# Attention and MoE on one core: other PSUM banks for the score blocks, transposes and value products, and weight passes at other places

## Chip, cores and metric

The kernel runs on one core of one Trainium2 chip. The metric is the device time of one execution in microseconds (us). The time before is the median of three runs.

## What is computed

Attention over 4 batches, 8 heads, 576 positions and head size 64, with a bias that a small network makes from relative positions, and behind it a two-layer MLP with a rational activation. Cut to what matters:

```python
scores = scale * q @ k.transpose(0, 1, 3, 2)
x = (psi_rel / psi_i)[..., None]
bias = maximum(x @ w1 + b1, 0) @ w2
scores = scores + bias.transpose(2, 0, 1)[None]
attn = exp(scores - max(scores)); attn = attn / (sum(attn) + 1e-9)
x = (attn @ v) as [2304, 512]
h = x @ w_in                                 # 512 -> 2048
g = (a0 + a1*h + a2*h^2 + a3*h^3) / (1 + |b0|*|h| + |b1|*h^2 + 1e-6)
out = g @ w_out                              # 2048 -> 512
```

## The kernel before

**Stages.** First the bias tables are made (to about 49 us), 36 groups `n` of 16 rows: rectified rows on VectorE and ScalarE, products with w2 on TensorE (L769), a read-out by ScalarE (L775), and a DMA to DRAM, from which bias tiles are read back. Then attention (to about 275 us), then the MLP. All of PSUM is one tile `W` of 8 banks with 512 columns of fp32; a helper `on` (L99) tells the dependency tracker which banks an instruction touches, so that waits between engines go by bank. Every engine works in the order in which the program is written; nothing reorders it.

**Attention.** A pair of heads of one batch is a unit (16 of them), and 128 query rows of it are a step; the last 64 rows of two units make one step together, so that there are 72 steps. A step `i` has two score blocks, `j` = 0 and 1, one per head, of 128 rows and 576 columns. `rnd(r)` (L599) writes one round: the scores of steps `i` = 2r and `i+1`, and what follows for the steps `i-1`, `i-2` and `i-3`:

- `e_qk` (L335): score products q·k (L346), two per block. The heads lie on different halves of the rows of the array and are woven together. A block is 576 wide and a bank 512, so before the change a block lay in a strip across two banks (`strip`, L332), cut into 448 and 128 columns; the four strips of a round shared banks 4 and 1.
- `e_ttr` (L359): the reduction. VectorE adds the bias to the score block and takes the row extreme in one custom instruction (L365), followed by a read of its accumulator. It writes `s2` and `m`.
- `e_exp` (L373): exponentials on ScalarE (L380), from `s2` to `prob`.
- `e_tp` (L426): transposes of `prob` on TensorE (L432), 16 `main` ones and 2 `ends` (the last 64 columns) per step, and, for units that end, `adds` (their row sums). `copy` (L446) brings the main ones from PSUM to `pt` by ScalarE (L447); `put_tails` (L454) brings ends and sums to `tl` and `rt` by VectorE.
- `e_pv` (L480): value products (L491), 20 per step, and `put` (L498), by which VectorE copies the output from PSUM to `xs` (L500).

A round's order on TensorE is: scores, transposes of step i-2, transposes of i-1, value products of i-3, value products of i-2.

**Weight passes.** Rounds 4 to 33 also split the MLP's weights into a high and a low part, two jobs `a` and `b` in every three rounds (`job_plan`, L567; phase `ph`): the mask pass `mag` (L156, VectorE), `rebias` (L165, ScalarE), `sign` (L168, VectorE), `mid` (L177, GpSimd), `join` (L181, VectorE), `low` (L188, GpSimd), and stores of the high part (`hi`) and the low one (`out`). `plan` says at which place of the round each is written:

```python
if ph == 0:
    plan.update(first=a[1], act=a[2], pool2=[a[4]], third=[a[3][0], hi(a)])
elif ph == 1:
    plan.update(first=b[1], act=b[2], second=[a[3][1]], pool2=[a[3][2]], outs=[out(c)])
else:
    plan.update(
        first=[b[3][0]], pool=[b[4]], second=[b[3][1]], pool2=[b[3][2]],
        outs=[hi(b), out(c + 1)],
    )
```

Here `a[1]` is mag, `a[2]` rebias, `a[3]` = sign, join, low, store, and `a[4]` mid. `first` stands ahead of the reductions of step i, behind the last put; `second` between the reductions of i and those of i+1; `third` and `outs` at the round's end.

**Start and end.** `start(0)` and `start(1)` (L662) write scores, reductions and exponentials of steps 0 and 1 behind the table groups y = 33 and y = 35. `finish` (L670) writes the last transposes and products and the first product of the MLP.

Of the kernel before, what the change touches and what calls it, by code (L numbers as in the profile page):

```python
# [37 lines left out]
def tile_attn_moe(  # L38
# [194 lines left out]
    with tc.manual_schedule():  # L233
# [3 lines left out]
        with ExitStack() as actx:  # L237
# [89 lines left out]
            MAIN_A, MAIN_B = 128, S - 128  # L327

            def low_first(i, j):
                return (i + j) % 2 == 0  # L330

            def strip(i, j):  # L332
                return 3 * 512 * (1 - j) + (512 - MAIN_B if low_first(i, j) else 1024 - MAIN_A)

            def e_qk(i):  # L335
# [6 lines left out]
                def product(j, a, z):  # L342
                    r, o0 = slice(64 * j, 64 * j + 64), strip(i, j)
# [6 lines left out]
                cuts = [(MAIN_A, S), (0, MAIN_A)], [(0, MAIN_B), (MAIN_B, S)]  # L350
                return [
                    [
                        (5 * (z - a) // 3, lambda j=j, a=a, z=z: product(j, a, z))
                        for a, z in cuts[low_first(i, j)]
                    ]
                    for j in range(2)
                ]

            def e_ttr(i, j):  # L359
                u, c = steps[i]  # L360
                p, b = units[u]
                t = epool.tile([P, S], F32, tag="s2", name=f"s2_{i}_{j}", bufs=4)
                m = epool.tile([P, 1], F32, tag="m", name=f"m{i}_{j}", bufs=8)
                o0 = strip(i, j)
                op = on(V.tensor_tensor_reduce(  # L365
                    out=t, in0=WF[:, o0:o0 + S], in1=bias[p][:, 5 * j + c, :],
                    scale=-0.125, scalar=3.0e38,
                    op0=ALU.add, op1=ALU.min, accum_out=m,
                ), o0 // 512, o0 // 512 + 1)
# [56 lines left out]
            def e_tp(i, to, tails, us=()):  # L426
# [11 lines left out]
                for r in range(2):  # L438
# [4 lines left out]
                    ends.append([op(r, tails[r], 128 + 64 * (i % 2), pb[:, 512:512 + P])])  # L443
                    adds.append([op(r, tails[r], 256, sums[u % 4]) for u in us])
# [9 lines left out]
            def put_tails(i, n, tails, us):  # L454
# [3 lines left out]
                for r, b in enumerate(tails):  # L458
                    on(V.tensor_copy(  # L459
                        out=t[:, k:k + n, 64 * r:64 * r + 64],  # L460
                        in_=W[:, b, 128 + 64 * k:128 + 64 * (k + n)].rearrange("p (k s) -> p k s", s=64),
                    ), b, mem=(f"tl{i // 2 % 2}",))
                for u in us:
# [3 lines left out]
                    for r, b in enumerate(tails):  # L467
                        on(V.tensor_copy(out=rt[0:n, 64 * r:64 * r + 64], in_=W[0:n, b, 256:320]), b)
# [98 lines left out]
            def job_plan(r):  # L567
                q, ph = divmod(r - 4, 3)
                c = 2 * q
                plan = {k: [] for k in ("first", "act", "pool", "second", "pool2", "third", "outs")}  # L570
# [26 lines left out]
            ZZ = (4, 1)  # L597

            def rnd(r):  # L599
# [21 lines left out]
                for j in range(2):  # L621
                    op = e_ttr(i, j)
                for x in plan["second"]:
                    op = x()
                for x in plan["pool2"]:
                    behind(x(), op)
# [25 lines left out]
                for x in plan["third"] + list(hi[1:]) + plan["outs"]:  # L652
                    x()
# [16 lines left out]
            def finish():  # L670
                run(puts)
                main, ends, _, copy = e_tp(NS - 2, (6, 7), ZZ)
# [8 lines left out]
                main, ends, adds, copy = e_tp(NS - 1, (5, 0), ZZ, us)  # L681
# [8 lines left out]
                put = e_pv(NS - 1, 5)  # L690
# [6 lines left out]
            with ExitStack() as bctx:  # L697
# [56 lines left out]
                for y, n in enumerate(order):  # L754
# [6 lines left out]
                    pa = (6, 7) if y == NG - 2 else (2 * ((y + 2) % 4), 2 * ((y + 2) % 4) + 1)  # L761
# [50 lines left out]
        with ExitStack() as mctx:  # L812
# [14 lines left out]
            def hb(s):  # L827
                return 2 - 2 * (s % 2), 3 - 2 * (s % 2)

            OB = (4, 5, 6, 7)  # L830
# [254 lines left out]
```

## Time and profile before

| | |
|---|---|
| median of three runs | 676.18 us (672.44 to 678.76) |
| the profiled execution | 674.15 us, span 672.4 us |
| TensorE busy (matmul) | 657.0 us, 98% of the span |
| VectorE busy | 554.0 us, 82% |
| ScalarE busy | 474.8 us, 71% |
| GpSimd busy | 153.2 us, 23% |
| granted TensorE clock | full speed in the whole span |

The profiled execution is 1.8 us longer than its span, which runs from the first to the last instruction. Matmuls are pipelined and overlap in the records, so a stop of TensorE appears as idle only in the part that is longer than the end of the matmul before it. Busy shares are means over the three stages; a round of attention has to be read by itself.

### The profile page before, as it was taken

Reading aid. Unit: us, or ns where it says so; the run is one execution under the profiler, and the core shown is the slowest. Engines: PE = TensorE matmul, PEld = TensorE weight load, DVE = VectorE, ACT = ScalarE, POOL = GpSimd, SP = SyncE. Lnnn points to the kernel's source line nnn. Section 1 sums busy time; section 2 is a strip of 40 time slices with the busy share of each in tenths; the row PEclk is TensorE's granted clock in tenths of the full one; section 3 lists DMA queues with packets and bytes.
Section 4 is the critical chain, followed back from the end, with each engine's and each line's share of the span. In section 5 each row is a group of like instructions: output and inputs, shape, how many; then the busy total and the mean of one; then the engine's idle time right before and its main releaser. Section 6 shows DMA issues by size and latency. Waiting matters only on the chain.

```text
span 672.4 us, 16098 instructions
## 1 busy us (share of the span) xinstructions
PE 657.0 (98%) x6274; PEld 537.2 (80%) x6274; DVE 554.0 (82%) x1030; ACT 474.8 (71%) x758; POOL 153.2 (23%) x108
## 2 busy tenths in 40 slices
PE   9999999999999899999999999999999999999997
PEld 6657777777777677988888888899988888888996
DVE  7986878788778787599998989979769878687776
ACT  7988898889889798566766657666655656455451
POOL 0000134333342321032221221221221212212211
PEclk9999999999999999999999999999999999999999
DMA  6887788677977974442662625768531301303031
GB/s 241 287 310 224 273 253 272 214 253 233 312 246 234 310 235 140 149 143 95 182 210 77 229 86 178 220 234 288 189 128 48 126 0 63 109 13 114 0 110 47
DMA packets 74844, 118.97 MB, mean 177 GB/s; under 512 B 11904, under 2 KB 33808, under 8 KB 74768
## 3 DMA queue, kind: packets, MB, share of 16 engines
q1 hardware_dynamic: 74624, 117.79, 53.0%
q8 instruction: 49, 0.80, 0.5%
q14 instruction: 27, 0.22, 0.1%
q10 hardware_dynamic: 144, 0.16, 0.1%
HBM read 79.17 MB, written 35.61 MB: 171 GB/s over the span
## 4 chain that ended last, share of the span: by engine, by line
PE 66%; DVE 4%; DMA 3%; issue 1%; ACT 1%; SPq 0%; DVEq 0%
PE ps L316 29%; PE ps L914 29%; PE ps L491 3%; DVE s L365 3%; PE ps L346 2%; PE ps L432 2%; DMA ws<-wh 2%; DMA wx<-in_w_out_dram 1%; DVE xs L500 0%; ACT p L380 0%; DVE tl L459 0%; ACT pt L447 0%; DVE sum L390 0%; DVE m L365 0%; DVE wk L156 0%
## 5 line engine op out<-in xcount | busy, mean ns | idle before, releaser
L884 POOL TENSOR_TENSOR gl<-m,r 128x1024 fp32r<-128x1024 f32 (+1 forms) x39 | 85.6, 2194 | 299.9 <-DVE m L877 243.9
L365 DVE CUSTOM_DVE_ANT_0 s<-ps,bias 128x576 f32<-128x576 f32 x144 | 105.6, 753 | 42.6 <-PE ps L346 33.2
L835 ACT ACTIVATE w<-ps,babs 128x1024 f32<-128x1024 f32 (+1 forms) x40 | 41.3, 1032 | 106.0 <-PE ps L316 102.3
L380 ACT ACTIVATE p<-s,m 128x576 f32<-128x576 f32 x144 | 110.1, 773 | 2.6 <-DVE m L365 2.6
L447 ACT COPY pt<-ps 128x512 f32<-128x512 f32 (+1 forms) x109 | 74.4, 727 | 22.7 <-PE ps L432 22.2
L346 PE MATMUL ps<-k,q 64*128 64x448 f32 (+3 forms) x640 | 89.8, 425 | 0.2 <-DVE m L365 0.2
L914 PE MATMUL ps<-wol,gh 128*128 128x512 f32 x216 | 84.2, 390 | 0.0
L914 PE MATMUL ps<-woh,gh 128*128 128x512 f32 x216 | 84.2, 390 | 0.0
L491 PE MATMUL ps<-pt,v 128*64 128x128 f32 (+1 forms) x1280 | 78.2, 265 | 1.8 <-ACT pt L447 1.8
L847 DVE SCALAR_TENSOR_TENSOR u<-w,babs,ps 128x1024 f32<-128x1024 f32 (+1 forms) x40 | 46.9, 1172 | 37.0 <-ACT t L836 36.8
L432 PEld LDWEIGHTS ps<-ident,p 64*128 64x128 f32 x1296 | 49.8, 138 | 28.0 <-DVE m L365 10.6
L491 PEld LDWEIGHTS ps<-pt,v 128*64 128x64 f32 x1280 | 65.1, 137 | 6.7 <-ACT pt L447 2.2
L316 PE MATMUL ps<-xb,wih 128*128 128x512 f32 (+1 forms) x240 | 68.7, 367 | 0.0
L842 ACT ACTIVATE u<-u 128x1024 f32<-128x1024 f32 (+1 forms) x40 | 39.1, 978 | 41.7 <-DVE u L847 41.5
L432 PE MATMUL ps<-ident,p 64*128 64x64 f32 x1296 | 55.0, 225 | 7.4 <-DVE m L365 6.4
L346 PEld LDWEIGHTS ps<-k,q 64*128 64x128 f32 (+1 forms) x640 | 43.5, 176 | 21.7 <-issue 16.6
L863 DVE SCALAR_TENSOR_TENSOR gh<-t,cst,r 128x1024 fp32r<-128x1024 f32 (+1 forms) x40 | 47.0, 1175 | 9.4 <-ACT r L844 7.0
L914 PE MATMUL ps<-woh,gl 128*128 128x512 f32 x216 | 53.8, 389 | 0.0
L870 DVE SCALAR_TENSOR_TENSOR m<-u,qc,gh 128x1024 f32<-128x1024 f32 (+1 forms) x40 | 47.1, 1178 | 5.1 <-DVE gh L863 1.4
L316 PEld LDWEIGHTS ps<-xb,wih 128*128 128x128 f32 x240 | 44.5, 188 | 6.0
L877 DVE SCALAR_TENSOR_TENSOR m<-t,cst,m 128x1024 f32<-128x1024 f32 (+1 forms) x40 | 47.1, 1178 | 1.4
L856 DVE SCALAR_TENSOR_TENSOR t<-t,cst,ps 128x1024 f32<-128x1024 f32 (+1 forms) x40 | 47.0, 1175 | 1.4
(81 smaller groups left out, 1319.8 us busy)
## 6 DMA issues: line engine op xcount, KB each, us to landing
tab<-e SPq DMA_DIRECT2D x36, 295.5 KB, 3.3
wx<-in_w_in_dram SPq DMA_DIRECT2D x16, 512.0 KB, 5.1
wx<-in_w_out_dram SPq DMA_DIRECT2D x16, 512.0 KB, 4.9
v<-in_vp_dram SPq DMA_DIRECT2D x16, 320.0 KB, 5.4
ws<-wh SPq DMA_DIRECT2D x20, 256.0 KB, 2.0
ws<-wl SPq DMA_DIRECT2D x20, 256.0 KB, 3.4
q<-in_qt_dram SPq DMA_DIRECT2D x16, 288.0 KB, 4.4
k<-in_kt_dram SPq DMA_DIRECT2D x16, 288.0 KB, 4.4
```

Source lines behind the costliest of these rows:

```text
L316: on(T.matmul(hps[s][:, j, :w_], w[:, k, sl], x[:, k, :w_], start=(k == 0 and z == 0), stop=(k == KD - 1 and z == 2),), b + j)
L346: on(T.matmul(WF[o, o0 + a:o0 + z], q[r, x], k[r, a:z], start=True, stop=True), (o0 + a) // 512)
L365: op = on(V.tensor_tensor_reduce(out=t, in0=WF[:, o0:o0 + S], in1=bias[p][:, 5 * j + c, :], scale=-0.125, scalar=3.0e38, op0=ALU.add, op1= ...
L380: A.activation(out=prob[i][:, z * S:z * S + S], in_=t, func=AF.Exp, bias=m, scale=-1.0, accum_out=sums[u % 4][:, k:k + 1],)
L432: on(T.transpose(W[:, b, o:o + 64], src[x, :], ident[x, x]), b)
L447: on(A.copy(out=t.rearrange("p x (r s) -> p r x s", r=2)[:, a:z], in_=W[:, to[a]:to[a] + z - a].rearrange("p r (x s) -> p r x s", s=64),), ...
L491: on(T.matmul(ps[y, o], vt[n][:, kc, y], w_, start=(kc == 0), stop=(kc == 4)), b, mem=(f"pt{i % 3}", f"tl{i // 2 % 2}"))
L856: on(V.scalar_tensor_tensor(out=rt[s, "t"], in0=rt[s, "t"], scalar=abs_[:, 1:2], in1=hp(s), op0=ALU.add, op1=ALU.mult,), *hb(s), mem="t")
L870: V.scalar_tensor_tensor(out=m, in0=rt[s, "u"], scalar=qc, in1=rt[s, "gh"].bitcast(F32), op0=ALU.add, op1=ALU.mult,)
L877: V.scalar_tensor_tensor(out=m, in0=rt[s, "t"], scalar=abs_[:, 0:1], in1=m, op0=ALU.add, op1=ALU.subtract)
L884: eng.tensor_tensor(out=lo, in0=rt[s, "m"], in1=rt[s, "r0"], op=ALU.mult)
L914: on(T.matmul(po[n, c], l[:, j, c * P:(c + 1) * P], r[fp][:, j, :], start=(first and x is a), stop=(last and x is z),), OB[c])
```

## The change

Each score block gets a pair of banks of its own, half of its columns (288) in each bank. `side(i)` gives the four banks of a step: one step of a round lies in banks 0 to 3, the other in 4 to 7, and the sides are swapped every round. With `b` the side of step i and `o` that of step i+1, the transposes of step i-2 go into (b, b+1) and those of i-1 into (b+2, b+3), which step i's reductions have read; tails and sums go behind the score columns of (o+1, o+3); the value products of i-3 and i-2 go into b+1 and b. All four score blocks stand at the round's start, both reductions of step i+1 stand ahead of the tail copies, and the places of the weight passes are four instead of seven. In the last two table groups, in `finish` and in the MLP only bank numbers change (MLP: first products in banks 0, 1 and 4, 5 instead of 0 to 3, second ones in 2, 3, 6, 7 instead of 4 to 7).

```diff
-                b = 2 - 2 * (s % 2)
+                b = 4 - 4 * (s % 2)
...
-            def strip(i, j):
-                return 3 * 512 * (1 - j) + (512 - MAIN_B if low_first(i, j) else 1024 - MAIN_A)
+            def side(i):
+                return 4 * ((i // 2 + i) % 2)
...
+                def product(j, a):
+                    r, b = slice(64 * j, 64 * j + 64), side(i) + 2 * j + a
                     for n, x, o in ops:
                         q, k = qk[n]
                         on(T.matmul(
-                            WF[o, o0 + a:o0 + z], q[r, x], k[r, a:z], start=True, stop=True
-                        ), (o0 + a) // 512)
+                            W[o, b, :SH], q[r, x], k[r, a * SH:(a + 1) * SH], start=True, stop=True
+                        ), b)
...
                 op = on(V.tensor_tensor_reduce(
-                    out=t, in0=WF[:, o0:o0 + S], in1=bias[p][:, 5 * j + c, :],
+                    out=t.rearrange("p (a s) -> p a s", a=2),
+                    in0=W[:, b:b + 2, :SH],
+                    in1=bias[p][:, 5 * j + c, :].rearrange("p (a s) -> p a s", a=2),
...
                 if ph == 0:
-                    plan.update(first=a[1], act=a[2], pool2=[a[4]], third=[a[3][0], hi(a)])
+                    plan.update(first=a[1], act=a[2], pool=[a[4]], second=[a[3][0], hi(a)])
                 elif ph == 1:
-                    plan.update(first=b[1], act=b[2], second=[a[3][1]], pool2=[a[3][2]], outs=[out(c)])
+                    plan.update(
+                        first=[a[3][1]] + b[1], act=b[2], pool=[a[3][2], b[4]],
+                        second=[b[3][0], out(c), hi(b)],
+                    )
                 else:
-                    plan.update(
-                        first=[b[3][0]], pool=[b[4]], second=[b[3][1]], pool2=[b[3][2]],
-                        outs=[hi(b), out(c + 1)],
-                    )
+                    plan.update(first=[b[3][1]], pool=[b[3][2]], second=[out(c + 1)])
...
-                main, ends, adds, copy = e_tp(i - 2, (6, 7), ZZ, us)
-                main_, ends_, _, copy_ = e_tp(i - 1, (2, 3), ZZ)
-                weave(sa[0] + sb[0][:1], sa[1] + sb[1][:1])
-                if not plan["pool"] and norms:
+                b, o = side(i), side(i + 1)
+                ZZ = (o + 1, o + 3)
+                main, ends, adds, copy = e_tp(i - 2, (b, b + 1), ZZ, us)
+                main_, ends_, _, copy_ = e_tp(i - 1, (b + 2, b + 3), ZZ)
+                weave(sa[0] + sb[0], sa[1] + sb[1])
+                if len(plan["pool"]) < 2 and norms:
...
-                weave(
-                    main[0] + small[0] + main_[0] + sb[0][1:],
-                    main[1] + main_[1] + small[1] + sb[1][1:],
-                )
+                weave(main[0][:4] + small[0] + main[0][4:] + main_[0], main[1] + small[1] + main_[1])
                 copy(1, 2)
                 copy(0, 1)
                 copy_(0, 2)
-                e_ttr(i + 1, 0)
+                for j in range(2):
+                    e_ttr(i + 1, j)
                 put_tails(i - 2, 2, ZZ, us)
-                e_ttr(i + 1, 1)
-                put = e_pv(i - 3, 7) if i > 2 else None
-                puts.append(e_pv(i - 2, 6))
+                put = e_pv(i - 3, b + 1) if i > 2 else None
+                puts.append(e_pv(i - 2, b))
...
-                    pa = (6, 7) if y == NG - 2 else (2 * ((y + 2) % 4), 2 * ((y + 2) % 4) + 1)
+                    pa = 2 * ((y if y >= NG - 2 else y + 2) % 4)
+                    pa = (pa, pa + 1)
```

TensorE in the round of steps 32 and 33, before. `k7` and `q7` make scores, `p30` and `p31` are the probabilities of steps 30 and 31, `pt` and `tl` their transposed copies, `v6` the values.

```order
L346 MATMUL ps_91<-k7_2136,q7_2135 128x448 x2
L346 MATMUL ps_91<-k7_2136,q7_2135 128x128 x2
L346 MATMUL ps_91<-k7_2136,q7_2135 128x448 x2
L432 MATMUL ps_91<-ident_60,p30_2585 128x64 x17
L432 MATMUL ps_91<-ident_60,p31_2588 128x64 x16
L432 MATMUL ps_91<-ident_60,p30_2585 128x64
L432 MATMUL ps_91<-ident_60,p31_2588 128x64 x2
L346 MATMUL ps_91<-k7_2136,q7_2135 128x128 x2
L491 MATMUL ps_91<-pt29_2486,v6_2022 64x128 x8
L491 MATMUL ps_91<-tl28_2553,v6_2022 64x128 x2
L491 MATMUL ps_91<-pt30_2612,v6_2022 64x128 x8
L491 MATMUL ps_91<-tl30_2674,v6_2022 64x128 x2
```

The same round after the change:

```order
L341 MATMUL ps_91<-k7_2138,q7_2137 128x288 x8
L422 MATMUL ps_91<-ident_60,p30_2586 128x64 x10
L422 MATMUL ps_91<-ident_60,p31_2589 128x64
L422 MATMUL ps_91<-ident_60,p30_2586 128x64 x8
L422 MATMUL ps_91<-ident_60,p31_2589 128x64 x17
L481 MATMUL ps_91<-pt29_2488,v6_2022 64x128 x8
L481 MATMUL ps_91<-tl28_2557,v6_2022 64x128 x2
L481 MATMUL ps_91<-pt30_2612,v6_2022 64x128 x8
L481 MATMUL ps_91<-tl30_2677,v6_2022 64x128 x2
```

The last two narrow scores have moved from behind the transposes to the others at the round's start, so that the value products follow directly on the transposes; of these, the ends have moved between the main ones of step 30. A row here is one product of the program; in the records each score or value product is two instructions.

VectorE from the end of that round into the next, before. `xs6` is written by puts, `wh4`, `wk4` and `wm4` by sign, mask pass and join; `s2_34_0` is the reduction of step 34's first block, followed by the read of its accumulator.

```order
L500 COPY xs6_2574<-ps_91 128x128
L168 SCALAR_TENSOR_TENSOR wh4_0_2610<-wx4_0_2250,wh4_0_2610 128x512
L500 COPY xs6_2574<-ps_91 128x128
L156 TENSOR_SCALAR wk4_1_2718<-wx4_1_2476 128x512
L365 ISA s2_34_0_2730,m34_0_2731<-ps_91,bias1_911 128x576
L365 ISA m34_0_2731 128x1
L365 ISA s2_34_1_2733,m34_1_2734<-ps_91,bias1_911 128x576
L365 ISA m34_1_2734 128x1
L181 SCALAR_TENSOR_TENSOR wm4_0_2628<-wm4_0_2628,wh4_0_2610 128x512
L365 ISA s2_35_0_2781,m35_0_2782<-ps_91,bias1_911 128x576
L365 ISA m35_0_2782 128x1
L459 COPY tl32_2784<-ps_91 128x2x64 x2
```

The same place after the change:

```order
L490 COPY xs6_2575<-ps_91 128x128
L168 SCALAR_TENSOR_TENSOR wh4_0_2610<-wx4_0_2250,wh4_0_2610 128x512
L490 COPY xs6_2575<-ps_91 128x128
L181 SCALAR_TENSOR_TENSOR wm4_0_2622<-wm4_0_2622,wh4_0_2610 128x512
L156 TENSOR_SCALAR wk4_1_2719<-wx4_1_2477 128x512
L353 ISA s2_34_0_2736,m34_0_2737<-ps_91,bias1_911 128x576
L353 ISA m34_0_2737 128x1
L353 ISA s2_34_1_2739,m34_1_2740<-ps_91,bias1_911 128x576
L353 ISA m34_1_2740 128x1
L353 ISA s2_35_0_2783,m35_0_2784<-ps_91,bias1_911 128x576
L353 ISA m35_0_2784 128x1
L353 ISA s2_35_1_2786,m35_1_2787<-ps_91,bias1_911 128x576
```

Join (L181) has moved from between the reductions of steps 34 and 35 to ahead of step 34's, before the mask pass, and the four reductions follow each other.

## Rows read from the trace of the kernel before

**Rows 1.** Busy us of each engine in two stretches: PE, PEld, DVE, ACT, POOL.

```profile
150.00:200.00 50.00, 48.54 (x820) 38.06 (x818) 41.05 (x131) 44.65 (x95) 18.50 (x15) 1.00 0.82 264
...
300.00:350.00 50.00, 50.00 (x222) 41.41 (x221) 48.43 (x51) 33.22 (x37) 11.75 (x6) 1.00 0.55 181
```

**Rows 2.** Timeline of TensorE, round of steps 32 and 33: start, us, what, [idle before].

```profile
142.33 2.00 PE L346 MATMUL ps<-k,q 64*128 64x448 f32 x12
144.16 0.78 PE L432 MATMUL ps<-ident,p 64*128 64x64 f32 x20
145.21 0.71 PE L432 MATMUL ps<-ident,p 64*128 64x64 f32 x16 [0.27 <-DVE m L365]
145.76 0.44 PE L346 MATMUL ps<-k,q 64*128 64x128 f32 x4
146.13 1.09 PE L491 MATMUL ps<-pt,v 128*64 128x128 f32 x16
...
148.14 0.39 PE L491 MATMUL ps<-tl,v 128*64 128x128 f32 x4
148.46 2.00 PE L346 MATMUL ps<-k,q 64*128 64x448 f32 x12
```

**Rows 3.** Timeline of VectorE, the same round and the start of the next.

```profile
143.71 0.76 DVE L365 CUSTOM_DVE_ANT_0 s<-ps,bias 128x576 f32<-128x576 f32 x1 [0.57 <-PE ps L346]
...
144.40 0.75 DVE L365 CUSTOM_DVE_ANT_0 s<-ps,bias 128x576 f32<-128x576 f32 x1
...
146.34 0.76 DVE L365 CUSTOM_DVE_ANT_0 s<-ps,bias 128x576 f32<-128x576 f32 x1 [1.18 <-PE ps L346]
...
149.19 0.27 DVE L500 COPY xs<-ps 128x128 f32<-128x128 f32 x1
149.39 0.41 DVE L156 TENSOR_SCALAR wk<-wx 128x512 uint32<-128x512 uint32 x1
149.84 0.76 DVE L365 CUSTOM_DVE_ANT_0 s<-ps,bias 128x576 f32<-128x576 f32 x1
```

**Rows 4.** Timeline of ScalarE: copies with a weight pass, that pass, copies without one.

```profile
144.86 2.10 ACT L447 COPY pt<-ps 128x512 f32<-128x512 f32 x3 [0.29 <-PE ps L432]
...
149.91 0.71 ACT L165 ACTIVATE wh<-wk,wmin 128x512 uint32<-128x512 uint32 x1
...
157.20 2.10 ACT L447 COPY pt<-ps 128x512 f32<-128x512 f32 x3 [1.05 <-PE ps L432]
```

**Rows 5.** Groups by line and shape, 68.41 to 255.32 us: busy us, mean ns, idle before.

```profile
L346 PE MATMUL ps<-k,q 64*128 64x448 f32 x213 | 52.5, 566 | 0.0
...
L447 ACT COPY pt<-ps 128x512 f32<-128x512 f32 x60 | 32.2, 589 | 16.1 <-PE ps L432 16.0
...
L346 PE MATMUL ps<-k,q 64*128 64x128 f32 x212 | 21.9, 284 | 0.0
...
L459 DVE COPY tl<-ps 128x128 f32<-128x128 f32 x60 | 14.5, 284 | 0.0
...
L500 DVE COPY xs<-ps 128x128 f32<-128x128 f32 x53 | 14.2, 272 | 2.7 <-ACT pt L447 1.0 <-PE ps L491 0.8 <-ACT p L380 0.8
L181 DVE SCALAR_TENSOR_TENSOR wm<-wm,wh 128x512 uint32<-128x512 uint32 x20 | 13.8, 691 | 0.0
L168 DVE SCALAR_TENSOR_TENSOR wh<-wx,wh 128x512 uint32<-128x512 uint32 x20 | 13.6, 679 | 0.1
```

**Rows 6.** Timeline, one round at 222 us: ScalarE waits for a store, TensorE for ScalarE.

```profile
226.75 0.72 ACT L165 ACTIVATE wh<-wk,wmin 128x512 uint32<-128x512 uint32 x1 [2.93 <-DMA ws<-wh]
...
228.00 1.09 PE L491 MATMUL ps<-pt,v 128*64 128x128 f32 x16 [1.56 <-ACT pt L447]
```

**Rows 7.** Timeline of the start: last two table read-outs, scores of steps 1 to 3, first value products.

```profile
48.98 1.37 ACT L775 ACTIVATE e<-ps,cst 128x591 f32<-128x591 f32 x2
...
49.22 2.58 PE L346 MATMUL ps<-k,q 64*128 64x448 f32 x14
...
54.89 1.09 PE L491 MATMUL ps<-pt,v 128*64 128x128 f32 x16 [0.27 <-ACT pt L447]
```

More of the change, by code (lines that the diff above doesn't have):

```diff
@@ L340, in e_qk @@
                     ops = [(u + z, slice(512, S), slice(64 * z, 64 * z + 64)) for z in range(2)]
-                def product(j, a, z):
-                    r, o0 = slice(64 * j, 64 * j + 64), strip(i, j)
+                def product(j, a):
+                    r, b = slice(64 * j, 64 * j + 64), side(i) + 2 * j + a
                     for n, x, o in ops:
@@ L346, in product @@
                         on(T.matmul(
-                            WF[o, o0 + a:o0 + z], q[r, x], k[r, a:z], start=True, stop=True
-                        ), (o0 + a) // 512)
[L350 to L357, printed above, removed]
+                            W[o, b, :SH], q[r, x], k[r, a * SH:(a + 1) * SH], start=True, stop=True
+                        ), b)
+                return [[(480, lambda j=j, a=a: product(j, a)) for a in range(2)] for j in range(2)]
             def e_ttr(i, j):
                 u, c = steps[i]
-                p, b = units[u]
+                p, _ = units[u]
                 t = epool.tile([P, S], F32, tag="s2", name=f"s2_{i}_{j}", bufs=4)
                 m = epool.tile([P, 1], F32, tag="m", name=f"m{i}_{j}", bufs=8)
-                o0 = strip(i, j)
+                b = side(i) + 2 * j
                 op = on(V.tensor_tensor_reduce(
-                    out=t, in0=WF[:, o0:o0 + S], in1=bias[p][:, 5 * j + c, :],
+                    out=t.rearrange("p (a s) -> p a s", a=2),
+                    in0=W[:, b:b + 2, :SH],
+                    in1=bias[p][:, 5 * j + c, :].rearrange("p (a s) -> p a s", a=2),
                     scale=-0.125, scalar=3.0e38,
                     op0=ALU.add, op1=ALU.min, accum_out=m,
-                ), o0 // 512, o0 // 512 + 1)
+                ), b, b + 1)
                 s2[i, j] = (t, m)
@@ L442, in e_tp @@
                     ])
-                    ends.append([op(r, tails[r], 128 + 64 * (i % 2), pb[:, 512:512 + P])])
-                    adds.append([op(r, tails[r], 256, sums[u % 4]) for u in us])
+                    ends.append([op(r, tails[r], SH + 64 * (i % 2), pb[:, 512:512 + P])])
+                    adds.append([op(r, tails[r], SH + P, sums[u % 4]) for u in us])
                 def copy(a, z):
@@ L467, in put_tails @@
                     for r, b in enumerate(tails):
-                        on(V.tensor_copy(out=rt[0:n, 64 * r:64 * r + 64], in_=W[0:n, b, 256:320]), b)
+                        on(V.tensor_copy(out=rt[0:n, 64 * r:64 * r + 64], in_=W[0:n, b, SH + P:SH + P + 64]), b)
                     nc.sync.dma_start(out=rsum[u], in_=rt[0:n])
@@ L569, in job_plan @@
                 c = 2 * q
-                plan = {k: [] for k in ("first", "act", "pool", "second", "pool2", "third", "outs")}
+                plan = {k: [] for k in ("first", "act", "pool", "second")}
                 if r < 4 or c >= len(jobs):
@@ L621, in rnd @@
                 for j in range(2):
[L622 to L626, printed above, removed]
+                    e_ttr(i, j)
                 small = [ends[r] + ends_[r] + adds[r] for r in range(2)]
-                weave(
-                    main[0] + small[0] + main_[0] + sb[0][1:],
-                    main[1] + main_[1] + small[1] + sb[1][1:],
-                )
+                weave(main[0][:4] + small[0] + main[0][4:] + main_[0], main[1] + small[1] + main_[1])
                 copy(1, 2)
@@ L651, in rnd @@
                     put()
-                for x in plan["third"] + list(hi[1:]) + plan["outs"]:
+                for x in plan["second"] + list(hi[1:]):
                     x()
@@ L671, in finish @@
                 run(puts)
+                ZZ = (1, 3)
                 main, ends, _, copy = e_tp(NS - 2, (6, 7), ZZ)
@@ L680, in finish @@
                 us = ended(NS - 1)
-                main, ends, adds, copy = e_tp(NS - 1, (5, 0), ZZ, us)
+                main, ends, adds, copy = e_tp(NS - 1, (0, 2), ZZ, us)
                 weave(*(main[r] + ends[r] + adds[r] for r in range(2)))
@@ L689, in finish @@
                 put.pop(0)()
-                put = e_pv(NS - 1, 5)
+                put = e_pv(NS - 1, 2)
                 done_to(NS)
@@ L827, in hb @@
             def hb(s):
-                return 2 - 2 * (s % 2), 3 - 2 * (s % 2)
-            OB = (4, 5, 6, 7)
+                return 4 - 4 * (s % 2), 5 - 4 * (s % 2)
+            OB = (2, 3, 6, 7)
             def rat0(s):
```

6 lines of the change are left out of this document (1 added, 5 removed).

## Prediction

> **What bounds the kernel now.** I read the stretches first. From 300 us on TensorE is busy for the whole stretch; between 150 and 200 us, inside the 35 attention rounds, it is busy 48.54 of 50 us [rows 1]. That end of the kernel is untouched by the change (only bank numbers differ), so what can be won lies in the rounds, and a busy share of 97% hides how a round is made. So I read next the timeline of TensorE over one round, that of steps 32 and 33 [rows 2], and beside it VectorE [rows 3] and ScalarE [rows 4]. Times below are counted from the round's first score matmul (142.33).
>
> TensorE: scores from 0; the first twenty transposes at 1.83; then a stop, the other sixteen transposes only at 2.88; the narrow scores at 3.43; the value products at 3.80; the next round at 6.13 [rows 2]. The stop is shown as 0.27 us of idle, but twenty transposes are followed by sixteen that take 0.55 to issue, so twenty should take about 0.6: the sixteen could have started at 2.43 and lose 0.45.
>
> What ends it: VectorE's two reductions of step 32 start at 1.38 and 2.07, and the transposes restart 0.81 after the second one's start (144.40 to 145.21) [rows 2, 3]. The diff's old strips say why: step 32's second block ends in banks 1 and 2, which the transposes and tails of step 31 are to overwrite. So a round today is a chain: first reduction at S, then 0.69 to the second, 0.81 to the restart, 0.55 + 0.37 + 2.33 to the next round, S + 4.75, with S = 1.38: 6.13, as seen. In the next round, where the weight passes come in between, S is 1.38 again (148.46 to 149.84) [rows 2, 3].
>
> **The change, part by part.**
>
> 1. *Scores.* A block of 448 + 128 columns becomes two of 288, still eight products (sixteen instructions) a round. The two shapes cost 566 and 284 ns, mean 425; a straight line between them puts 288 columns at 425 too [rows 5]. Bounds: nothing, or what the narrow ones lose by standing alone: four of them hold TensorE 0.37 us [rows 2], and scaled from the wide part (1.83 us for 448 + 128 + 448 columns) 128 columns are 0.23, so at most 0.14 gained a round. All scores now stand together and end at 1.83 x 1152/1024 = 2.06. I take no gain from shape; the place is what counts (next).
>
> 2. *Where the transposes wait.* Step i-2's now go into the pair that step i's first block left, so they wait for the FIRST reduction: S + 0.81 = 2.19, against 2.06 when the scores end. That exposes 0.13. Step i-1's wait for the second reduction, S + 1.50 = 2.88, and the first twenty take until 2.19 + 0.61 = 2.80: 0.08 more. They end at 3.43.
>
> 3. *A new wait for ScalarE.* The narrow scores stood between the transposes and the value products and hid ScalarE's first copy. It starts 0.70 after the first transpose (144.16 to 144.86) [rows 2, 4] and takes 0.59 [rows 5]; the product into that bank follows perhaps 0.05 later. So the products start at 2.19 + 0.70 + 0.59 + 0.05 = 3.53, not 3.43, and the round ends at 3.53 + 2.33 = 5.86. In terms of S: S + 4.48, which is 0.27 less than S + 4.75.
>
> 4. *Reductions of step i+1* no longer wait for narrow scores. They wait for the tails in their banks (about 2.8 and 3.0), run until 4.3, the tail copies until 4.7, and the second product needs the tails at about 5.6. Hidden by the products, 0.9 us of room.
>
> 5. *Weight passes.* 'Join' (L181, 691 ns) moves from between the reductions to ahead of them. In one round of three it stands before the mask pass. There VectorE starts its put when the products are done, 0.07 into the round (148.14 + 0.39) and some 0.08 of signal later; then put 0.20 (149.19 to 149.39), join 0.69, mask pass 0.45 (149.39 to 149.84) [rows 2, 3, 5]: S = 1.49, 0.11 later. Bounds: 0 (all done before the scores are) to 0.69 (the whole pass). I take 0.11, near the lower end, because each part has a row. In the second kind of round join takes the place of the sign pass of the same length: 0. Behind a late pass stand the four reductions, and for them wait the transposes.
>
> 6. *The read of two half banks.* The reduction now reads 2 x 288 in two stretches. Not in this trace; nearest: copies of 128 elements in two stretches take 284 ns, in one 272 [rows 5]. So 0 to 0.012 us each; below zero by at most as much, since the old strip crossed a bank border too. I take 0.
>
> 7. *Store one round earlier.* The high half of the second job is stored a round earlier. Once in the trace ScalarE's pass over weights waits 2.93 us for such a store, and TensorE 1.56 us behind it [rows 6]. That goes, I take 1.6; bound 0, if another store comes late instead. The store is issued by SyncE, in order: it now waits there for the sign pass at the round's end, and the next round's loads stand behind it, a round or more ahead of their use. GpSimd's two passes and the normalization change places too; it is busy 18.50 of 50 us [rows 1] and only join and the stores wait for it. Both: 0.
>
> 8. *The start.* Step 1 now lies in banks 4 to 7, in which the last two table groups are. ScalarE reads those out in 48.98 to 50.35 [rows 7], so step 1's second block starts at 50.4, where today its scores run from 49.22. And round 1's first scores need the same banks, so they wait for both reductions. Worked on with the same parts: reductions of step 1 at 51.2 and 51.9, step 2's scores from 52.0 and 52.7, its reduction at 53.6, transposes at 54.65, two copies, first value product about 56.5 instead of 54.89: 1.6 lost. Bounds 0.5 (half of it hidden) to 2.5.
>
> **Sum.** Rounds 2 to 34 are 33; ten of them have the longer S. 23 x 0.27 + 10 x 0.16 = 7.8 us. In two of the last rounds ScalarE has casts on top and gives nothing back: 0.5 less, 7.3. Stores 1.6, start -1.6. Against the profiled execution's 674.15 us that is 666.9; the median of the three runs stands 2.03 higher, so I predict **668.9**, 1.1% less. About 1% (6.8 us) is what a measurement here can tell from no change, so the forecast lies on that border.
>
> **Rivals.**
>
> *ScalarE takes the bound.* From one round's copies to the weight pass are 5.05 us (144.86 to 149.91), and that pass is 0.71: 5.76 in two rounds of three. Before, it idled 0.29 us ahead of the copies in a round with that pass and 1.05 in one without [rows 4]; 0.27 shorter rounds leave 0.02 in the first kind. For: so little is left. Against: no idle is needed, only order. If those twenty rounds lose 0.2 each, 4 us of the gain go: 673.
>
> *The wait comes back at the first transposes.* Today they go to a pair nobody reads; now to the one VectorE has just read. If S + 0.81 becomes S + 1.08, nothing is won in the rounds: 676. For: it is the same kind of hand-over as the one removed. Against: the scores of step i+1 cover all but 0.13 of it.
> The Trainium skill, Perfetto Trace Analysis, Matmuls, speaks for this rival: independent groups should rotate through different banks, so that the read of one overlaps the matmuls of the next. By that rule the new place is the worse one and the time would not fall; the rows agree that it is a wait, but a short one.
>
> *Slower: VectorE becomes the bound.* It is busy 41.05 of 50 us [rows 1], 5.03 of a round's 6.13; two each of join 0.69, sign 0.68 and mask 0.45 in three rounds are 1.21 of that, so 3.82 without them. The rounds that now hold all three have 3.82 + 1.82 = 5.64, nearly the 5.9 of the new round. If such a round also keeps the waits that VectorE shows today (0.57 and 1.18 us [rows 3]), it takes 7.4, and ten of them cost 10 x 1.27 = 13 instead of giving 1.6: 668.9 + 14.3, about 683. It decides once the put starts later than about 0.7 into a round, for then the scores of step i+1, which need the bank it reads, stop as well. For: today's put does start 0.73 in (149.19). Against: it is late there because the reductions of step i+1 are; those come 1.2 us sooner now.
>
> *More than forecast.* If the copy is hidden, only the chain through step i-1's transposes is left, S + 4.38, and a round gains 0.37: 33 x 0.1 more, 665.6.
>
> **How the numbers follow.** Forecast 0.56, more 0.14, ScalarE 0.12, wait comes back 0.08, slower 0.10. The forecast's own range is 665 to 672; 0.34 of its 0.56 lies below 669.4 (1% under the median), with the 0.14: faster 0.48. The rest of it, 0.22, with 0.12 and 0.08: same 0.42. Slower 0.10. The range, 662 to 678, leaves out the slower case and some of the tail below; its ends are "more" without the loss at the start (665.6 - 1.6 = 664) and "comes back" (676), each with some 2 us for the scatter of runs.
>
> **What would show it.** Rounds of 5.8 to 5.95 us, from first score to first score; transposes starting about 2.2 in and a second, short stop before the last sixteen at most; value products released by ScalarE's copy, not by VectorE; VectorE's wait for narrow scores (1.18) gone; ScalarE's idle before copies under 0.1 in weight rounds; the first value product near 56.5. I am wrong if rounds stay above 6.1, if the put starts later than 0.7 in, or if the scores of step i+1 are seen waiting for a put.

## The result, and the profile after

| | before | after |
|---|---|---|
| median | 676.18 us (5 runs, 672.44 to 678.76) | 667.55 us (5 runs, 667.49 to 668.57) |
| the profiled execution | 674.15 us, span 672.4 | 668.14 us, span 666.4 |
| ratio of the mean times (95% interval) | 1 | 0.9887 (0.9847 to 0.9927) |

Faster by 1.1%, and the interval does not reach 1. To read the scatter: executions of the kernel before have a mean granted TensorE clock of 0.999 or 1.000 (35 of the 64 beside the experiments: median 673.29 us) or of 0.994 to 0.997 (29 of them: median 675.66 us); all five of the changed kernel had 0.994 to 0.997. The profiled executions differ by 6.0 us.

TensorE in the round of steps 32 and 33, timeline of the changed kernel: start, us, what, idle before. It answers to [rows 2].

```profile
143.11 2.21 PE L341 MATMUL ps<-k,q 64*128 64x288 f32 x16
145.32 1.39 PE L422 MATMUL ps<-ident,p 64*128 64x64 f32 x36
146.71 1.09 PE L481 MATMUL ps<-pt,v 128*64 128x128 f32 x16
...
148.73 0.39 PE L481 MATMUL ps<-tl,v 128*64 128x128 f32 x4
149.05 2.21 PE L341 MATMUL ps<-k,q 64*128 64x288 f32 x16
```

The round takes 5.94 us (before 6.13). The stop between the transposes of [rows 2] is gone: all 36 stand in one row, and the value products follow at 3.60, in the records 0.05 behind the end of ScalarE's first copy. But a short stop ahead of the transposes, 2.21 into the round, is hidden in the row of scores, since a stop shows only beyond the end of the matmul before it. Single score records start 0.24 us apart (two side by side), the last at 1.80, so the transposes could have started near 2.05. The weight loads (PEld) show what they wait for, and VectorE the end of the first reduction, the read of its accumulator:

```profile
145.31 1.25 PEld L422 LDWEIGHTS ps<-ident,p 64*128 64x128 f32 x36 [0.45 <-DVE m L353]
```

```profile
145.18 0.08 DVE L353 DVE_READ_ACCUMULATOR2_ANT m<- 128x1 f32 x1
```

The transposes start 0.06 us behind the end of this read, in 23 of the 33 rounds between the first scores of rounds 2 and 35, this one among them. So the hand-over now costs about 0.16 us.

VectorE in that round and the start of the next, as in [rows 3]:

```profile
144.50 0.76 DVE L353 CUSTOM_DVE_ANT_0 s<-ps,bias 128x576 f32<-128x576 f32 x1 [0.57 <-ACT p L370]
...
145.94 0.76 DVE L353 CUSTOM_DVE_ANT_0 s<-ps,bias 128x576 f32<-128x576 f32 x1
...
149.23 0.29 DVE L490 COPY xs<-ps 128x128 f32<-128x128 f32 x1 [0.20 <-PE ps L481]
149.44 0.68 DVE L181 SCALAR_TENSOR_TENSOR wm<-wm,wh 128x512 uint32<-128x512 uint32 x1
150.04 0.42 DVE L156 TENSOR_SCALAR wk<-wx 128x512 uint32<-128x512 uint32 x1
150.43 0.76 DVE L353 CUSTOM_DVE_ANT_0 s<-ps,bias 128x576 f32<-128x576 f32 x1
```

The wait of 1.18 us for narrow scores is gone. Put, join and mask pass now fit ahead of the next round's reduction: put starts 0.18 into the round (149.23), the reduction 1.38 (150.43), as before.

ScalarE's copies in two rounds with a weight pass and one without, as in [rows 4]:

```profile
146.07 1.99 ACT L437 COPY pt<-ps 128x512 f32<-128x512 f32 x3 [0.31 <-PE ps L422]
...
152.00 1.99 ACT L437 COPY pt<-ps 128x512 f32<-128x512 f32 x3 [0.30 <-PE ps L422]
...
157.99 1.99 ACT L437 COPY pt<-ps 128x512 f32<-128x512 f32 x3 [0.97 <-PE ps L422]
```

Its idle time ahead of the copies is about what it was (0.29 and 1.05), though the round is 0.19 shorter: three copies take 1.99 us, before 2.10.

Busy us in the stretch of [rows 1], and two groups over the whole span (busy us, mean ns, idle before):

```profile
150.00:200.00 50.00, 49.98 (x846) 40.57 (x844) 42.71 (x134) 45.28 (x99) 19.42 (x16) 1.00 0.82 259
```

```profile
L353 DVE CUSTOM_DVE_ANT_0 s<-ps,bias 128x576 f32<-128x576 f32 x144 | 103.4, 755 | 19.4 <-PE ps L341 6.2 <-ACT p L370 5.2 <-PE ps L422 3.7
...
L341 PE MATMUL ps<-k,q 64*128 64x288 f32 x512 | 75.6, 426 | 2.0 <-ACT e L760 1.5 <-DVE m L353 0.5
```

The start, in answer to [rows 7]: last table read-outs, scores of steps 1 to 3, first value products, and below them stretches of 2 us there (columns as in [rows 1]; the one behind POOL is the granted clock).

```profile
48.42 1.37 ACT L760 ACTIVATE e<-ps,cst 128x591 f32<-128x591 f32 x2
49.20 1.88 PE L341 MATMUL ps<-k,q 64*128 64x288 f32 x8 [1.46 <-ACT e L760]
51.57 4.33 PE L341 MATMUL ps<-k,q 64*128 64x288 f32 x15 [0.49 <-DVE m L353]
...
57.79 1.09 PE L481 MATMUL ps<-pt,v 128*64 128x128 f32 x16 [0.54 <-ACT pt L437]
```

```profile
48.00:50.00 2.00, 0.80 (x4) 0.45 (x6) 0.00 (x0) 1.79 (x4) 0.00 (x0) 1.00 0.63 238
...
52.00:54.00 2.00, 2.00 (x10) 1.36 (x10) 0.61 (x3) 1.27 (x5) 0.00 (x0) 0.58 0.06 12
54.00:56.00 2.00, 2.00 (x16) 1.35 (x13) 1.11 (x4) 0.00 (x0) 0.00 (x0) 0.57 0.94 289
```

The first value product comes 2.90 us later than before (54.89). TensorE, idle 1.46 us and then 0.49 us, is granted 0.58 and then 0.57 of its clock from 52 to 56 us, near the lower of its two levels (1.2 of 2.4 GHz), and the scores of steps 2 and 3 take 4.33 us there.

**Where the time went.** Between the first scores of rounds 2 and 35 lie 33 rounds: 205.24 us before (56.21 to 261.45), 197.36 after (59.03 to 256.39), 7.88 less, the vanished stop behind a store included. The start gives 2.82 back; from there to the end 0.94 is gained. Sum 6.0.

### The profile page after: what moved, and what is told of

The parts are those of the page before. It is cut to its first block, busy times and chain, and to the rows that moved or that the text cites. A ratio compares the mean times of both kernels' runs of the same rounds, so it can differ in the third digit from the quotient of the medians.

```text
span 666.4 us, 16107 instructions
## 1 busy us (share of the span) xinstructions
PE 657.5 (99%) x6274; PEld 544.5 (82%) x6274; DVE 558.5 (84%) x1030; ACT 471.6 (71%) x758; POOL 153.0 (23%) x108
## 4 chain that ended last, share of the span: by engine, by line
PE 93%; ACT 2%; DVE 2%; DMA 1%; issue 1%; SPq 0%; POOL 0%; DVEq 0%; ACTq 0%; POOLq 0%
PE ps L316 30%; PE ps L899 30%; PE ps L481 11%; PE ps L341 10%; PE ps L754 6%; PE ps L422 6%; ACT p L370 1%; DVE s L353 1%; DMA rs<-rt 1%; ACT pt L437 1%; PE ps L706 1%; DMA rb<-rs 0%; DVE xs L490 0%; ACT e L760 0%; SPq L389 0%
## 5 line engine op out<-in xcount | busy, mean ns | idle before, releaser
L353 DVE CUSTOM_DVE_ANT_0 s<-ps,bias 128x576 f32<-128x576 f32 x144 | 103.4, 755 | 19.4 <-PE ps L341 6.2
L437 ACT COPY pt<-ps 128x512 f32<-128x512 f32 (+1 forms) x109 | 71.8, 731 | 22.8 <-PE ps L422 22.8
L341 PE MATMUL ps<-k,q 64*128 64x288 f32 (+1 forms) x640 | 84.6, 424 | 2.0 <-ACT e L760 1.5
L341 PEld LDWEIGHTS ps<-k,q 64*128 64x128 f32 (+1 forms) x640 | 52.0, 178 | 23.7 <-issue 5.6
L422 PEld LDWEIGHTS ps<-ident,p 64*128 64x128 f32 x1296 | 45.9, 138 | 15.5 <-DVE m L353 14.2
L422 PE MATMUL ps<-ident,p 64*128 64x64 f32 x1296 | 50.8, 226 | 0.9 <-DVE m L353 0.6
```

Source lines behind the costliest of these rows:

```text
L341: on(T.matmul(W[o, b, :SH], q[r, x], k[r, a * SH:(a + 1) * SH], start=True, stop=True), b)
L353: op = on(V.tensor_tensor_reduce(out=t.rearrange("p (a s) -> p a s", a=2), in0=W[:, b:b + 2, :SH], in1=bias[p][:, 5 * j + c, :].rearrange( ...
L422: on(T.transpose(W[:, b, o:o + 64], src[x, :], ident[x, x]), b)
L437: on(A.copy(out=t.rearrange("p x (r s) -> p r x s", r=2)[:, a:z], in_=W[:, to[a]:to[a] + z - a].rearrange("p r (x s) -> p r x s", s=64),), ...
```

## The experiments

Each is made from the changed kernel if nothing else is said. The table has lengths of two successive rounds and the mean of the 33, all differences between starts of a round's first score in the profiles; in the second round join stands ahead of the reductions wherever the passes have their new places.

| kernel | median us | ratio to before (interval) | steps 32, 33 | steps 34, 35 | mean |
|---|---|---|---|---|---|
| before | | | 6.13 | 6.21 | 6.22 |
| changed | 667.55 | 0.9887 (0.9847 to 0.9927) | 5.94 | 6.00 | 5.98 |
| passes back | 669.48 | 0.9932 (0.9902 to 0.9961) | 5.93 | 6.00 | 6.03 |
| passes only | 678.25 | 1.0052 (1.0034 to 1.0070) | 6.13 | 6.68 | 6.37 |
| 128 columns late | 677.85 | 1.0056 (1.0035 to 1.0077) | 6.13 | 6.57 | 6.31 |
| 288 columns late | 687.47 | 1.0198 (1.0160 to 1.0235) | 6.38 | 6.84 | 6.57 |
| start moved | 664.67 | 0.9853 (0.9823 to 0.9883) | 5.93 | 6.00 | 5.96 |
| output elsewhere | 672.23 | 0.9954 (0.9931 to 0.9977) | 5.96 | 6.23 | 6.10 |
| both of these | 669.31 | 0.9929 (0.9905 to 0.9954) | 5.97 | 6.22 | 6.08 |
| start moved, passes back | 670.45 | 0.9930 (0.9903 to 0.9958) | 5.92 | 6.01 | 6.00 |

**Passes back.** `job_plan` and its places in `rnd` are those of before (one of the three phases shown):

```diff
                 elif ph == 1:
+                    plan.update(first=b[1], act=b[2], second=[a[3][1]], pool2=[a[3][2]], outs=[out(c)])
...
-                        first=[a[3][1]] + b[1], act=b[2], pool=[a[3][2], b[4]],
-                        second=[b[3][0], out(c), hi(b)],
...
```

> The changed kernel with the weight passes in the rounds where they were before (join between the two reductions of the one step and the other, cast and GpSimd passes in their old rounds, one GpSimd product or pass per round, store issued a round later). Theory of the hand-over (the gain comes from scores that all go out at the round's head into banks of their own, and no longer wait behind the transposes): rounds stay near the changed kernel's 5.94 to 6.00 us, only the 1.6 us stall on the store comes back, so 668 to 671 us. Rival (the new places of the passes give the gain): 673 to 676 us, rounds of 6.1 us and more.

669.48 us, as the hand-over has it. Nearly all rounds are the changed kernel's to 0.02 us; in three, of 6.17, 7.41 and 6.62 us, TensorE stops behind ScalarE, which waits for a store, and three others are 0.12 to 0.58 us shorter than in the changed kernel. So the new places of the passes shorten no plain round; they take stops for stores away, and cost a little in single rounds.

**Passes only.** The kernel before with the changed kernel's `job_plan` and places.

> The kernel before with nothing changed but the rounds and places of the weight passes, which are the changed kernel's; strips of 448 and 128 columns and the shared banks stay. Theory of the hand-over: rounds stay near 6.2 us, since TensorE still sends the late scores after the transposes; only the store's stall of 1.6 us goes, so 673 to 677 us. Rival (the passes give the gain): 668 to 671 us.

678.25 us, outside both ranges: the passes alone cost 0.5%. Timelines of TensorE and VectorE in the round of steps 34 and 35:

```profile
151.10 2.00 PE L346 MATMUL ps<-k,q 64*128 64x448 f32 x12
152.93 0.66 PE L432 MATMUL ps<-ident,p 64*128 64x64 f32 x16
153.78 0.34 PE L432 MATMUL ps<-ident,p 64*128 64x64 f32 x4 [0.18 <-DVE m L365]
...
154.45 0.65 PE L432 MATMUL ps<-ident,p 64*128 64x64 f32 x14 [0.28 <-DVE m L365]
```

```profile
151.83 0.28 DVE L500 COPY xs<-ps 128x128 f32<-128x128 f32 x1
152.03 0.68 DVE L181 SCALAR_TENSOR_TENSOR wm<-wm,wh 128x512 uint32<-128x512 uint32 x1
152.63 0.42 DVE L156 TENSOR_SCALAR wk<-wx 128x512 uint32<-128x512 uint32 x1
152.96 0.75 DVE L365 CUSTOM_DVE_ANT_0 s<-ps,bias 128x576 f32<-128x576 f32 x1
```

Put starts 0.73 into the round, as in the kernel before, where VectorE's reductions of the round before wait for the late scores [rows 3]; with join behind it the reduction starts at 1.86 instead of 1.38. Join fits ahead of the reductions only where those come early.

**128 columns late.** Own pairs and new passes stay; the cut is 448 and 128 again, and step i+1's 128-column products go behind the transposes. The tail copies go back ahead of step i+1's reductions, so that the value products don't wait for those.

```diff
-                weave(sa[0] + sb[0], sa[1] + sb[1])
+                weave(sa[0] + sb[0][:1], sa[1] + sb[1][:1])
...
-                weave(main[0][:4] + small[0] + main[0][4:] + main_[0], main[1] + small[1] + main_[1])
+                weave(
+                    main[0][:4] + small[0] + main[0][4:] + main_[0] + sb[0][1:],
+                    main[1] + small[1] + main_[1] + sb[1][1:],
+                )
...
+                put_tails(i - 2, 2, ZZ, us)
                 for j in range(2):
                     e_ttr(i + 1, j)
-                put_tails(i - 2, 2, ZZ, us)
...
```

> The changed kernel, own bank pairs and new passes kept, but scores cut 448 and 128 again, and the 128-column products of the round's second step sent after the transposes (0.37 us of TensorE); VectorE copies the tails ahead of the second step's two reductions, so that the value products don't wait for those. Theory of the hand-over: the value products, which start 0.19 us after the transposes now, start 0.37 us after them, so each of 33 rounds is 0.16 to 0.19 us longer: 667.5 + 5.3 to 6.3 = 673 to 674 us. Rival (separate banks alone give the gain, whatever is sent when): 667 to 668.5 us.

677.85 us: direction right, size wrong. TensorE, plain round:

```profile
145.78 2.00 PE L341 MATMUL ps<-k,q 64*128 64x448 f32 x12
147.98 1.39 PE L421 MATMUL ps<-ident,p 64*128 64x64 f32 x36 [0.19 <-DVE m L354]
149.20 0.44 PE L341 MATMUL ps<-k,q 64*128 64x128 f32 x4
149.57 1.09 PE L480 MATMUL ps<-pt,v 128*64 128x128 f32 x16
...
151.91 2.00 PE L341 MATMUL ps<-k,q 64*128 64x448 f32 x12
```

The plain round is 0.19 longer, as expected (value products 3.79 in, not 3.60). The expectation left out that the round of steps 34 and 35 grows by 0.57: there the late scores push VectorE back, as in the run before. Passes only has the same late columns and the same places of the passes, but shared banks, and takes 678.25 us (mean round 6.37, here 6.31): own banks without the early scores gain next to nothing. Own banks with late scores and the old places of the passes were not run.

**288 columns late.** The same move with the 288-column halves.

> The changed kernel with its 288-column halves, but the second halves of the round's second step (0.55 us of TensorE) sent after the transposes, and the tails copied ahead of the second step's reductions. Theory of the hand-over: 0.55 less the 0.19 us that TensorE waits there anyway, times 33 rounds, is 11.9 us: 667.5 + 11.9 = 679 us (677 to 682), slower than the kernel before, whose late part was 0.37 us. Rival (separate banks alone give the gain): 667 to 668.5 us. If late 128 columns and late 288 columns cost the same, the length of the late part isn't what counts.

687.47 us, above the forecast of 677 to 682. The plain round is 0.44 longer (6.38), the other 0.84. The time rises with the length of the late part. That the order makes the round, and not the banks by themselves, is shown by these two runs and passes only; the banks are what allows the order.

**Start moved.** ScalarE issues step 0's exponentials behind the last table read-outs:

```diff
             def start(i):
...
-                for j in range(2):
-                    e_exp(i, j)
+                for k in range(4 * i):
+                    e_exp(k // 2, k % 2)
```

> The changed kernel with one move at the start: ScalarE issues step 0's two exponentials after the read-outs of the last two table groups, not ahead of them, so that the banks in which step 1's scores go come free about 1.5 us sooner (two exponentials of 0.78 us less). Theory of the start (the new bank plan makes step 1's first score wait 1.46 us for a read-out, and TensorE, idle there, is then granted a lower clock in some executions): the first value product 1.0 to 1.5 us sooner, and 666.0 to 666.5 us; if TensorE's clock also stays at full there, up to 1.7 us more, 664.5 us. Rival (the start is hidden behind something else, such as the bias loads or the later exponentials): 667 to 668 us, no change.

664.67 us, the best time of all and the theory's figure for a full clock. Start and granted clock:

```profile
48.69 1.23 PE L341 MATMUL ps<-k,q 64*128 64x288 f32 x6 [0.24 <-ACT e L760]
50.41 2.64 PE L341 MATMUL ps<-k,q 64*128 64x288 f32 x15 [0.49 <-DVE m L353]
...
54.95 1.09 PE L481 MATMUL ps<-pt,v 128*64 128x128 f32 x16 [0.55 <-ACT pt L437]
```

```profile
52.00:54.00 2.00, 2.00 (x43) 1.85 (x39) 1.77 (x5) 0.29 (x3) 0.00 (x0) 1.00 0.19 24
54.00:56.00 2.00, 1.46 (x31) 1.32 (x27) 1.52 (x6) 2.00 (x4) 0.00 (x0) 1.00 0.95 293
```

The stop of 1.46 us is 0.24, the clock stays at its upper level, and the first value product stands at 54.95, where it was before the change (54.89).

**Output elsewhere.** The round's first value product goes into free columns of the bank of a block of step i+1, not yet reduced:

```diff
-                put = e_pv(i - 3, b + 1) if i > 2 else None
+                put = e_pv(i - 3, o, SH) if i > 2 else None
```

> The changed kernel with the first value product of a round (step i-3) written to the free columns of the other side's bank instead of the second transposed bank, so that TensorE need not wait for ScalarE's first copy of it. Theory (in a round of 5.94 us TensorE's last 0.19 us of waiting is that copy): 0.19 us times 33 rounds, so 661 to 663 us, if VectorE and ScalarE keep up (ScalarE was idle 0.31 us in a round with a weight pass). Rival 1 (ScalarE's copies and exponentials bound the round already): 666.5 to 668 us, the wait only moves to the second value product. Rival 2 (a bank that VectorE reads while TensorE writes it costs both): over 668 us.

672.23 us, slower than the changed kernel by 4.7 and outside every range but the second rival's. TensorE, the value products of two rounds:

```profile
142.75 1.09 PE L481 MATMUL ps<-pt,v 128*64 128x128 f32 x16 [0.22 <-DVE m L353]
...
147.28 1.39 PE L422 MATMUL ps<-ident,p 64*128 64x64 f32 x36
148.72 1.09 PE L481 MATMUL ps<-pt,v 128*64 128x128 f32 x16
```

They now wait for VectorE's reduction of that bank's block instead of ScalarE's copy: in every round the first one starts 0.06 us behind the end of step i+1's first reduction, in about half of the rounds some 0.2 us later than in the changed kernel. So it is not a cost of a shared bank for both, as the second rival says, but the same hand-over at a later place. Whether 0.19 us a round can be had from ScalarE's copy is left open by it.

**Both.**

> The moves of the start and of the value product together in the changed kernel: if each is worth what its theory says and they don't touch, 667.5 less 1.3 less 5.5 is 660.7 us (659 to 662); if ScalarE bounds the round, 666 us.

669.31 us, above both forecasts: 2.9 less than the one before, 4.6 more than the start alone. The two moves do not disturb each other; the product's move costs here what it costs alone.

**Start moved, passes back.**

> The kernel of the moved start exponentials (664.67 us, TensorE's clock at full in its runs) with the weight passes back in the rounds of before: the size of the new places of the passes by itself, without the clock of the start in it. Theory of the hand-over with the store's stall as the passes' only part: 664.7 + 1.6 = 666.3 us (665.8 to 667). Rival (the passes are worth more in rounds whose reductions wait for them): 668 us or more.

670.45 us, from 666.11 to 668.11 at full clock (three of eleven executions; the lowest is 1.4 more than 664.67, as expected) to 674.4 (at 0.995). The median is the rival's figure, but plain rounds are as short as with the passes in their new places (5.92 and 6.01); what is added has to come from single rounds. The start alone was run again beside it:

> The kernel of the moved start exponentials once more, to see how often TensorE's clock falls there: its six executions all kept it, but four of ten of the kernel with the value product elsewhere as well, which has the same start, did not. If the move at the start keeps the clock, all executions are within 664.5 to 665.0 us; if it only makes the fall rarer, some stand near 667 us with a mean clock of 0.997.

664.74 us (664.47 to 666.74): one of six executions stood at 0.997. The move makes the fall of the clock rarer and doesn't rule it out.

> The same start with the passes in their old rounds once more, for a profile: its executions ran from 666.1 us at full clock to 674.4 us at 0.995. If the stop for the store is where the clock falls, the profile of an execution above 668 us shows a granted clock near 0.5 to 0.6 behind that stop (near 200 us); if it is the start, between 48 and 56 us. At full clock: 666 us and no answer.

671.2 us, with the answer in its profile: ScalarE waits for a store, TensorE for ScalarE, and then the granted clock falls.

```profile
224.40 0.72 ACT L165 ACTIVATE wh<-wk,wmin 128x512 uint32<-128x512 uint32 x1 [2.34 <-DMA ws<-wh]
```

```profile
225.65 1.50 PE L481 MATMUL ps<-pt,v 128*64 128x128 f32 x16 [2.09 <-ACT pt L437]
...
229.65 2.21 PE L341 MATMUL ps<-k,q 64*128 64x288 f32 x16
```

```profile
226.00:228.00 2.00, 2.00 (x24) 2.00 (x22) 0.29 (x1) 2.00 (x5) 0.00 (x0) 0.55 1.05 411
228.00:230.00 2.00, 2.00 (x21) 1.62 (x19) 0.18 (x1) 2.00 (x6) 0.00 (x0) 0.60 0.98 376
```

This round takes 9.63 us, 3.7 more than a plain one: 2.09 of stop, the rest at 0.55 to 0.60 of the clock. So a store that comes late can cost nearly twice its wait. This round and two others in which TensorE stops behind ScalarE (7.93 and 6.98 us), against 7.29, 6.19 and 5.88 in the execution of 666.11, hold the whole 5.1 us between the two.

## Why the prediction was right, and where its steps were off

The time (668.9 forecast, 667.55 measured) came out by the mechanism forecast, with three terms of the sum off: the rounds, the store and the start. That the figure lies so near is in part luck. The forecast fall was 7.3 us; the two profiles have 6.0, or 7.7 without the fall of TensorE's clock at the start, and the medians 8.6, because the median before (676.18) is a high one: that of the 64 executions beside the experiments is 674.5.

1. **Scores.** Forecast to end at 2.06, with no gain from shape. From the single records it is 2.05; the row of 2.21 holds the wait that follows. The mean of one is 426 ns, forecast 425. In two pieces before they took 2.20 (1.83 + 0.37), so one row is 0.15 shorter, near the bound of 0.14. The round gets none of it, since the transposes wait for the reduction.
2. **Transposes.** Forecast 2.19 for the first, released by the FIRST reduction, and 2.88 for the last sixteen, released by the second; measured 2.21 and, in the single records, 2.88. So the wait did not vanish: it moved to the first reduction and costs 0.16, forecast 0.13. The rival "the wait comes back" needed another 0.27 and fell, because the scores of step i+1 cover the rest of the hand-over. The Trainium skill, Perfetto Trace Analysis, Matmuls, wants independent groups in different banks so that a read overlaps the next matmuls. The trace agrees that a place with a reader just done is a wait, of 0.16 us, and the run with the output elsewhere, which put a product into a bank still to be read, agrees by 4.7 us.
3. **ScalarE's copy.** Forecast 0.70 + 0.59 + 0.05 behind the first transpose, products at 3.53; measured 0.75 + 0.59 + 0.05 and 3.60. The products follow ScalarE's copy, as forecast. The 0.70 is from [rows 2], where those transposes waited for nothing; the changed kernel has it too in the rounds of 5.88 us, in which they start when the scores end. Behind a stop the first transposes take 0.05 more, and this start-up the sum had at nothing. This is the mis-sized term: with 0.02 from the transposes, a plain round gained 0.19, not 0.27.
4. **Join ahead.** Forecast S = 1.49 and a gain of 0.16 in those rounds; measured 1.38 and about 0.2. The durations were added, but the passes start closer than they are long (join at 149.44, mask pass at 150.04).
5. **Store.** Forecast 1.6. The round of 8.06 us in the profile before became one of 5.88, where one of its kind takes 6.08 before: 1.98. In executions whose clock falls behind such a stop it is more (670.45 against 664.67).
6. **Start.** Forecast 1.6 lost. At full clock it is 1.23: the profile of the kernel with the passes back, whose start is the same, has the first value product at 56.12. In the changed kernel's profile 2.90, and the 1.67 between are the fall of TensorE's clock, which the prediction didn't have.
7. **The rest.** The two-stretch read costs nothing (755 ns against 753). The end gained 0.94, not forecast. In a single round after the change 0.58 was lost (last section).

In numbers: 33 rounds by 0.2 are 6.6, the store 2.0, the end 0.9, less 2.8 at the start and 0.6 in that round: 6.1, near the 6.0 of the two profiles; the forecast had 7.3 + 1.6 - 1.6.

ScalarE did not take the bound: its idle time, forecast under 0.1, stayed 0.30, and its three copies became 0.11 shorter. The slower rival did not happen in the changed kernel, where put starts 0.18 into the round; its condition, put later than about 0.7, did come about in the passes-only run (0.73, with the shared banks), and that run is slower than before, though by less than the rival's price.

## What to carry to other kernels

Read a round by what ends each wait, and ask what stands between the hand-over and its waiter: here independent products (step i+1's scores) ahead of the transposes hide all but 0.16 us of the hand-over, worth 0.2 us in each of 33 rounds, and work moved ahead of VectorE's reductions paid only once those came early. A pass that is harmless beside one change can cost time without it, so parts are tried alone and together. A row without idle time can still hold a wait: look at the weight loads and at the end of the instruction that may be waited for. Look also at the seams: stops of 1.5 to 2 us of TensorE, at the start or behind a store, cost 1.6 to 1.7 us more where the clock granted after them fell.

## What was not expected of the hardware

TensorE's clock fell behind stops of 1.46 and 0.49 us at the start (granted 0.58 and 0.57 from 52 to 56 us) and of 2.09 us in a round (0.55 to 0.60 from 226 to 230 us), to near 1.2 GHz, with TensorE busy throughout while it was low. It doesn't fall in every execution: the kernel with the passes back has the same stops of 1.46 and 0.49 us at the start, and full clock behind them in its profile:

```profile
51.59 2.64 PE L341 MATMUL ps<-k,q 64*128 64x288 f32 x15 [0.49 <-DVE m L353]
...
56.12 1.09 PE L481 MATMUL ps<-pt,v 128*64 128x128 f32 x16 [0.55 <-ACT pt L437]
```

Among kernels with the new start and no stop for a store (changed, 128 late, 288 late, output elsewhere) 11 of 29 executions had a mean clock of 0.999 or 1.000, with the start moved (start moved twice, both) 17 of 22. The passes-only kernel, with the old start and no stop for a store, had 0.999 or 1.000 in all 8; the kernel before, with a stop for a store, in 35 of 64. Short stops can be enough: the profile of both changes together has 0.24 and 0.49 us at the start and 0.50 granted from 52 to 54 us. What decides in one execution stays open.

In one round of the changed kernel VectorE's mask pass took 1.66 us instead of 0.42, beside a GpSimd product, and TensorE waited for it:

```profile
89.37 1.66 DVE L156 TENSOR_SCALAR wk<-wx 128x512 uint32<-128x512 uint32 x1
```

```profile
89.34 1.41 POOL L405 TENSOR_TENSOR xs<-xs,rb 128x576 f32<-128x576 f32 x1 [3.90 <-DMA rb<-rs]
```

```profile
91.77 1.39 PE L422 MATMUL ps<-ident,p 64*128 64x64 f32 x36 [0.57 <-DVE m L353]
```

The product ends at 90.75, and the pass ends 0.28 later. The Trainium skill, SBUF — State Buffer, "SBUF: two separate sides", says that VectorE and GpSimd share a pair of ports which one instruction, of certain kinds on VectorE, holds to its end while the other waits. The rows agree with it (the pass began 0.03 behind the product). So do seven other profiles in which this pass begins 0.10 to 0.78 us behind the start of such a product: it always ends 0.28 to 0.30 behind the product's end. The profile of both changes together, for example:

```profile
88.55 1.41 POOL L405 TENSOR_TENSOR xs<-xs,rb 128x576 f32<-128x576 f32 x1 [3.77 <-DMA rb<-rs]
89.29 0.95 DVE L156 TENSOR_SCALAR wk<-wx 128x512 uint32<-128x512 uint32 x1
```

In the three profiles with the passes back in their old rounds no mask pass begins under a product, and the round that took 6.51 us takes 5.93.
